# Pooled attention and a gated MLP on one core: another order of issue for the same blocks, and other engines for the steps that can stand on either of two

## The chip, the core and the metric

The kernel runs on one core of one Trainium2 chip. The metric is the time of one execution on the device in microseconds, of which less is better. The engines are named as in the profile: PE (TensorE: matmuls), PEld (its weight loads), DVE (VectorE), ACT (ScalarE), POOL (GpSimd) and SP (SyncE, which only issues transfers here). Each engine works through its own queue in the order in which the instructions were issued, and waits on semaphores for the others.

## What is computed

Attention over keys and values that are averaged by eight, for 8 batches, 8 heads, 576 rows and 64 columns a head; then on its output, read as 576 x 512 for each batch, a gated MLP that mixes rows with a 576 x 576 matrix. The weights arrive as 64-bit floats.

```python
def _attn_ref(q, k, v):
    k_p = k.reshape(B, H, Sp, pool, D).mean(axis=3)
    v_p = v.reshape(B, H, Sp, pool, D).mean(axis=3)
    scores = scale * np.matmul(q, k_p.transpose(0, 1, 3, 2))
    attn = np.exp(scores - np.max(scores, axis=-1, keepdims=True))
    attn = attn / (np.sum(attn, axis=-1, keepdims=True) + 1e-09)
    return np.matmul(attn, v_p)

def _moe_ref(x, w_in, g_ln, w_sg, b_sg, w_out):
    h = gelu_tanh(x @ w_in)
    u, v = h[..., :d_ff // 2], h[..., d_ff // 2:]
    v_n = (v - mean(v)) / np.sqrt(var(v) + 1e-06) * g_ln
    v_s = np.einsum('ts,bsd->btd', w_sg, v_n) + b_sg[None, :, None]
    return x + (u * v_s) @ w_out
```

## The kernel before

Nothing in the kernel loops over batches at run time: one program of 9779 profiled instructions is laid out in full. Its work is cut into steps, each a generator function with stages that end at a `yield`. A step has a letter, a number (the pair of heads g, a row tile i, or a column block d or m) and a batch b. The table `ORDER` (L27) names steps as `S2+3` (step S, pair 2, batch 3); `emit` (L770) goes through it and each time issues the next stage of that step. At the end every instruction is tied to the one before it on its engine, so the table is the order of issue on all engines and SyncE's queue. Where this text writes S2+3, it means that step.

The steps of a batch: A, B, C and E issue the loads of `kraw` (keys), `vraw`, `qT` and the values left over; K sums keys by eight into the block-diagonal `kbd`; P does so for the values (`vb` in batch 0, `vbh` and `vbl` later). S (L473) makes the scores of a pair of heads by five matmuls into a PSUM tile `aps`, the negated row maximum `nmax` (L486), the exps `e` and their sum `ssum`, and normalises. L and T transpose `e` and `el` (batch 0 on TensorE, later on VectorE and by a round trip of `tfar` through HBM) and split the result into a high part `ah` and a low part `al`. V multiplies with the values and copies PSUM to `xhl` and `x32` (named `x` in rows). J (batch 0) and H (a tile of 128 rows; H4 the 64 left over) make the v half of the first product, a gelu `vg`, its mean and variance, and the high and low parts `vhh`, `vhl` (`vht` for H4). U makes the u half. W (L684) mixes rows with `wsh`, `wsl`, `wth`, `wtl` and gates (`u`, L697, then `ghi` and `glo`). O multiplies with `w_out` (`woh`, `wol`) and adds `x` (L733, L721 in the last step). Z stores. Lower-case names are for the weights: `lv0` loads, `v0` to `v3`, `u0` to `u3`, `o0` to `o3` turn 64-bit words into a high and a low part (L275 to L283 and L222 to L231), `s0` to `s4` split the mixing matrix.

Two PSUM tiles `mps` go round between J, H, U, W and O, and two tiles `aps` between S, V and the transposes of batch 0; a step whose turn has come waits until the tile's last reader is done.

Some steps can stand on either of two engines. A key such as `m30` (kind of step, batch up to a cap, number) in the set `OTHER` takes the second:

```python
def copy(o, i, key):        # G ghi, h and x: V's copies, g vhh, s, T, P: VectorE if in OTHER, else ScalarE
def move(o, i, key):        # X, c: GpSimd if in OTHER, else ScalarE
def lower(o, x, y, key):    # with lowest: VectorE in one instruction if in OTHER, else ScalarE and GpSimd
def combine(o, x, y, op, key):  # V, H, W, s?d, v?d and the like: VectorE if in OTHER, else GpSimd
def sum8(o, t, key):        # k, p, l: one reduction on VectorE if in OTHER, else three sums on GpSimd
```

For the softmax three more: with `m` in `OTHER`, `soften` (L446) subtracts the maximum of the whole tile on VectorE (L448), `expo` (L451) is one exp on ScalarE (L453) and `total` (L460) one sum on VectorE (L462); without it, `expo` is ten exps with their own maximum and sum (L457), each followed by a read of the accumulator. With `n`, GpSimd normalises `e` (L443), without it VectorE, with the reciprocals kept in PSUM. With `z`, VectorE centres and scales `vg` in one instruction (L467), without it ScalarE does (L470, L471).

Exp and gelu lie in different tables of ScalarE. `ready` (L201) issues a one-column activation `early` (L204) where the function changes, with a table load ahead of it; how often that happens is set by the order.

Of the kernel before, what the change touches and what calls it, by code (L numbers as in the profile page):

```python
# [32 lines left out]
S0+1 J2+0 J3+0 H0+0 V3+0 C1+1 K1+1 o1 K0+2 C3+1 S1+1 H2+0 H2+0 C2+1 S2+1 K0+2 H0+0 H2+0 H1+0 s3 H0+0 H3+0 V1+0 H0+0
o0 s0 o0 H4+0 H2+0 H2+0 H0+0 S1+1 s1 H2+0 H3+0 o3 H4+0 B0+2 U0+0 H1+0 S2+1 H4+0 C0+2 S1+1 o2 A1+2 H3+0 o3 S2+1 o2 o2
S1+1 S1+1 U0+0 S0+1 o2 U1+0 U1+0 C1+2 o3 T0+1 P2+1 H1+0 H3+0 T0+1 S2+1 H4+0 S3+1 S3+1 S3+1 S0+2 o3 P2+1 S2+1 H4+0
T1+1 C2+2 U2+0 U2+0 S3+1 S3+1 s4 U3+0 S1+2 H3+0 H3+0 H4+0 H1+0 H1+0 L0+1 H4+0 H4+0 s4 T0+1 T2+1 U3+0 P2+1 S0+2 W0+0
W0+0 W0+0 S0+2 K1+2 L0+1 W1+0 W0+0 B1+2 P2+1 L0+1 W1+0 W1+0 L0+1 T0+1 W2+0 W2+0 P0+2 V0+1 V0+1 S1+2 P1+2 S1+2 W2+0
W2+0 T1+1 T1+1 L0+1 W3+0 W1+0 W3+0 O0+0 T1+1 V1+1 W3+0 C3+2 W3+0 T2+1 V1+1 V1+1 V1+1 T3+1 K1+2 S0+2 A0+3 S1+2 O1+0
O1+0 T2+1 T2+1 O0+0 O0+0 S2+2 V2+1 S0+2 V2+1 T0+2 T3+1 A1+3 O1+0 V2+1 E0+2 P2+2 O2+0 O3+0 S2+2 V0+1 S2+2 S2+2 T3+1
K0+3 S3+2 T3+1 O3+0 V2+1 O2+0 S3+2 S2+2 O2+0 V3+1 V3+1 V3+1 H0+1 H0+1 O3+0 Z3+0 H0+1 C1+3 H0+1 H1+1 H2+1 V3+1 S3+2  # L40
C0+3 H1+1 H1+1 S3+2 T0+2 T1+2 H0+1 H3+1 H2+1 S1+2 H0+1 K0+3 S0+3 H2+1 V0+1 Z2+0 H1+1 K1+3 H1+1 H4+1 S3+2 H3+1 H2+1
P2+2 H1+1 U0+1 L0+2 H4+1 H4+1 H3+1 H4+1 H4+1 T0+2 P2+2 P2+2 U1+1 U0+1 S1+3 L0+2 H3+1 Z0+0 H2+1 U1+1 C3+3 U2+1 S0+3
T0+2 P2+2 B0+3 L0+2 L0+2 H3+1 L0+2 V0+2 H4+1 H4+1 U3+1 T1+2 U2+1 U3+1 H2+1 H3+1 C1+4 H4+1 W0+1 T2+2 C2+3 S1+3 T1+2
S0+3 Z1+0 T1+2 V1+2 V0+2 T2+2 S1+3 W1+1 W0+1 V0+2 V1+2 V1+2 C0+4 K1+3 T3+2 P0+3 V0+2 S1+3 B1+3 A0+4 S2+3 T2+2 T2+2
S0+3 W1+1 V2+2 S2+3 S2+3 V2+2 V2+2 T3+2 K0+4 W2+1 W2+1 P1+3 E0+3 T3+2 S0+3 T0+3 W1+1 W1+1 W3+1 S3+3 T3+2 V3+2 W3+1
V3+2 V3+2 H0+2 W0+1 H0+2 T0+3 H1+2 K0+4 W0+1 T1+3 S3+3 S3+3 W2+1 H1+2 H2+2 S2+3 P2+3 V2+2 H2+2 C0+5 V1+2 W2+1 O0+1
W3+1 P2+3 S3+3 H0+2 T0+3 P2+3 P2+3 W3+1 S3+3 T0+3 V3+2 T2+3 P2+3 B0+4 S0+4 O0+1 O0+1 O1+1 O1+1 S2+3 S1+3 L0+3 O2+1
O2+1 H1+2 H0+2 H2+2 A1+4 H0+2 O1+1 H1+2 P0+4 H2+2 H1+2 H1+2 S1+4 H0+2 H3+2 O2+1 S0+4 S1+4 H3+2 L0+3 O3+1 C3+4 H3+2
H2+2 H4+2 L0+3 L0+3 C1+5 H4+2 A0+5 O3+1 V0+3 Z1+1 Z2+1 O3+1 H4+2 H4+2 Z0+1 C2+4 K1+4 Z3+1 E0+4 H4+2 S0+4 S0+4 U0+2
U0+2 U1+2 U1+2 H3+2 B1+4 T1+3 S0+4 T1+3 T1+3 H3+2 U2+2 H3+2 U2+2 P1+4 K0+5 H4+2 V1+3 H4+2 U3+2 T2+3 T2+3 L0+3 T3+3  # L50
U3+2 H2+2 V0+3 V0+3 H4+2 V1+3 S1+4 V0+3 P2+4 A1+5 W0+2 W1+2 T2+3 V2+3 W0+2 T3+3 W1+2 W1+2 V1+3 T3+3 V2+3 V2+3 V1+3
W2+2 T3+3 W3+2 W2+2 B0+5 W3+2 K1+4 K0+5 W2+2 W3+2 W1+2 V3+3 S2+4 T0+4 P2+4 V3+3 V3+3 H0+3 S1+4 S2+4 H1+3 H0+3 W0+2
W2+2 K1+5 H1+3 H1+3 H0+3 S2+4 W0+2 S3+4 H1+3 H1+3 S3+4 H2+3 H2+3 H2+3 W3+2 O0+2 O1+2 S1+4 O0+2 S2+4 S2+4 T0+4 T0+4
O0+2 O1+2 S0+5 S3+4 S3+4 O2+2 S1+5 T1+4 O2+2 S0+5 H2+3 S0+5 O1+2 H3+3 S3+4 L0+4 P2+4 T2+4 P0+5 H0+3 H1+3 V3+3 B1+5
H0+3 O2+2 H0+3 H3+3 H3+3 H3+3 H3+3 O3+2 O3+2 A0+6 T0+4 O3+2 V2+3 P2+4 Z2+2 S0+5 Z3+2 H4+3 H4+3 H4+3 L0+4 H4+3 H4+3
L0+4 U0+3 Z0+2 U0+3 P2+4 U1+3 L0+4 K0+6 V0+4 Z1+2 T1+4 S0+5 U1+3 K1+5 C2+5 L0+4 T3+4 S1+5 S1+5 S1+5 U2+3 U2+3 H3+3
T1+4 H2+3 U3+3 T1+4 V1+4 H2+3 U3+3 H4+3 E0+5 C1+6 C3+5 T2+4 P1+5 V0+4 V0+4 H4+3 T0+5 T2+4 H4+3 W0+3 W1+3 V1+4 W0+3
# [778 lines left out]
```

## Time and profile before

| | |
|---|---|
| median of 3 runs | 600.14 us (599.07 to 603.17) |
| the profiled execution, on the device | 599.96 us |
| its span, first to last instruction | 598.3 us |
| mean granted clock of TensorE | 0.973 |
| busy: PE, PEld | 546.6 us (91%), 506.7 us (85%) |
| busy: DVE, ACT, POOL | 415.6 us (69%), 318.4 us (53%), 274.2 us (46%) |
| moved by DMA | 67.10 MB |
| table loads on ACT | 43 at L204, 1283 ns each |

A timeline row gives the start and length in microseconds, the engine, the line, the operation, the tile written and the tiles read, the shapes and the number of like instructions merged; in brackets stands how long the engine had been idle and what ended that wait. A row by kind gives the count, then the busy time, the mean of one in ns, and the idle time ahead of it. Shares of the whole span are means over stretches with different limits, so the rows below go by stretch.

### The profile page before, as it was taken

The page shows a single profiled execution, that of the slowest core. Times are in us where ns is not written, and L with a number is a line of the kernel's source. Part 1 is how long each engine was busy: PE and PEld are TensorE (multiplying, and loading weights), DVE is VectorE, ACT ScalarE, POOL GpSimd, SP SyncE. Part 2 cuts the span into 40 slices and gives each one's busy share as a digit, 9 for nine tenths or more (in the row PEclk, how much of TensorE's full clock was granted, in tenths as well). Part 3 has the DMA queues.
Part 4 walks back from the last instruction along what each step waited for, and adds up shares of the span by engine and source line. Part 5 has one row for each costly group of instructions (what it writes and reads, how often), then busy time and mean ns, then how long its engine had stood idle before and what let it go on. Part 6 is the DMA issues. An engine that isn't in the chain of part 4 may idle for free. (4 is left out here: it accounts for less than half of the span.)

```text
span 598.3 us, 9779 instructions
## 1 busy us (share of the span) xinstructions
PE 546.6 (91%) x3552; PEld 506.7 (85%) x3552; DVE 415.6 (69%) x637; ACT 318.4 (53%) x833; POOL 274.2 (46%) x341
## 2 busy tenths in 40 slices
...
GB/s 288 389 173 60 146 114 80 135 121 127 92 207 132 66 125 253 81 93 16 178 169 100 76 65 157 133 85 99 82 132 31 79 1 101 79 100 40 1 1 80
DMA packets 43136, 67.10 MB, mean 112 GB/s; under 512 B 5776, under 2 KB 22160, under 8 KB 43088
## 3 DMA queue, kind: packets, MB, share of 16 engines
...
q10 hardware_dynamic: 288, 0.44, 0.3%
...
## 5 line engine op out<-in xcount | busy, mean ns | idle before, releaser
L133 PE MATMUL mps<-xhl,wih 128*128 128x288 f32 x512 | 91.2, 300 | 1.8 <-ACT u L681 1.1
L133 PE MATMUL mps<-wih,xhl 128*128 128x512 f32 x256 | 87.2, 410 | 5.0 <-DVE u L697 2.2
L133 PEld LDWEIGHTS mps<-xhl,wih 128*128 128x128 f32 x512 | 76.8, 192 | 3.4 <-ACT u L681 1.3
L443 POOL TENSOR_TENSOR e<-e,ssum 128x720 f32<-128x720 f32 x31 | 46.6, 1506 | 48.9 <-DVE ssum L442 33.9
L133 PEld LDWEIGHTS mps<-wih,xhl 128*128 128x128 f32 x256 | 49.4, 193 | 18.6 <-issue 2.0
L231 POOL TENSOR_TENSOR xhl<-x,xhl 128x576 fp32r<-128x576 f32 x23 | 35.5, 1550 | 58.4 <-ACT x L211 54.0
L133 PE MATMUL mps<-ghi,woh 128*128 128x288 f32 x240 | 53.3, 304 | 8.3 <-ACT vg L640 6.1
L457 ACT ACTIVATE e<-aps,nmax 128x72 f32<-128x72 f32 x180 | 54.7, 344 | 6.4 <-DVE nmax L486 6.3
L133 PE MATMUL mps<-xhl,wil 128*128 128x288 f32 x256 | 55.6, 298 | 0.0
L204 ACT ACT_TABLE_LOAD x43 | 55.2, 1283 | 0.7
L133 PE MATMUL mps<-wsh,vhl 128*128 128x288 f32 x256 | 55.0, 296 | 0.0
L133 PE MATMUL mps<-wsl,vhh 128*128 128x288 f32 x256 | 54.7, 295 | 0.0
L647 POOL TENSOR_TENSOR rstd<-mv,eps 128x1 f32<-128x1 f32 (+1 forms) x40 | 10.9, 274 | 95.4 <-DVE mv L645 84.0
L133 PE MATMUL mps<-wsh,vhh 128*128 128x288 f32 x256 | 54.6, 294 | 0.0
L133 PE MATMUL mps<-ghi,wol 128*128 128x288 f32 x240 | 52.0, 298 | 0.0
L133 PE MATMUL mps<-glo,woh 128*128 128x288 f32 x240 | 51.7, 297 | 0.0
L133 PE MATMUL mps<-wil,xhl 128*128 128x512 f32 x128 | 51.5, 403 | 0.0
L133 PEld LDWEIGHTS mps<-ghi,woh 128*128 128x128 f32 x240 | 39.1, 191 | 11.1 <-ACT vg L640 7.7
L695 DVE SCALAR_TENSOR_TENSOR mps<-mps,gcol,bbc 128x576 f32<-128x576 f32 x32 | 26.2, 817 | 27.0 <-PE mps L133 26.8
L231 POOL TENSOR_TENSOR glo<-u,ghi 128x576 fp32r<-128x576 f32 x15 | 24.6, 1649 | 42.1 <-ACT ghi L211 18.8
L644 DVE BATCH_NORM_STATS2 bst<-vg 128x6 f32<-128x512 f32 (+1 forms) x40 | 27.2, 680 | 23.1 <-ACT vg L640 21.1
L133 PE MATMUL aps<-kbd,qT 128*128 128x144 f32 x300 | 41.4, 286 | 1.6 <-ACT e L457 1.6
...
## 6 DMA issues: line engine op xcount, KB each, us to landing
qT<-in_q SPq DMA_DIRECT2D x31, 288.0 KB, 3.6
out<-x SPq DMA_DIRECT2D x31, 288.0 KB, 2.5
...
al<-tfar SPq DMA_DIRECT2D x28, 288.0 KB, 2.8
...
```

What stands on the lines that cost most here:

```text
L133: nc.tensor.matmul(o, lhsT, rhs, start=start, stop=stop)
L204: nc.scalar.activation(early, eps[:, 0:1], func)
L231: (nc.vector if key in OTHER else nc.gpsimd).tensor_tensor(o, x, y, op=op)
L443: (nc.gpsimd if key in OTHER else nc.vector).tensor_tensor(e, e, rec.unsqueeze(3).broadcast_to([P, NT, 2, SP]), op=ALU.mult)
L457: nc.scalar.activation(e[:, i, h], slots[i][:, h], AF.Exp, bias=nmax[:, i, h:h + 1], accum_out=ssum[:, i, h:h + 1])
L644: nc.vector.bn_stats(bst, vg)
L647: nc.gpsimd.tensor_tensor(rstd, mv[:, 1:2], eps[:n, 1:2], op=ALU.add)
L695: nc.vector.scalar_tensor_tensor(vs, vs, gcol[:, d:d + 1], bbc.rearrange("p (a n) -> p a n", a=2), op0=ALU.mult, op1=ALU.add)
```

## The change

Two tables are replaced: `ORDER`, with the same steps and stages in another sequence, and `OTHER`, from which 53 keys go and to which 43 come (104 instead of 114). No function is changed. A line of each table:

```diff
-E0+0 lv0 A0+0 A1+0 C0+0 C2+0 v0 H0+0 v0 v1 v1 K0+0 v0 v0 K1+0 K0+0 S0+0 S0+0 v1 v1 K1+0 C1+0 C3+0 S0+0 E0+1 P2+1
+A0+0 C0+0 E0+0 lv0 v1 v1 A1+0 K0+0 K0+0 S0+0 H0+0 H1+0 v1 C1+0 S1+0 B0+0 S0+0 K1+0 v1 S0+0 B1+0 A0+1 C2+0 S1+0 S1+0
-m30 m31 n00 n01 n02 n03 n10 n11 n12 n13 n20 n21 n22 n30 n31 n32 n33 o1d o1m o2a o2d o2m o3d o3m s2 s2d s3d s4 s4d
+c22 g00 g04 g10 g13 g14 g21 g22 g23 g24 h11 h20 k10 k31 l2 l3 m00 m02 m10 m12 m21 m22 m23 m30 m31 m32 m33 n00 n01
```

By engine: TensorE and SyncE keep their instructions. On ScalarE 150 of 200 single exps go and 15 whole-tile exps come; 14 table loads go, 29 stay; 15 casts of `ghi` come, 11 scalings of `vg` go. On VectorE 15 whole-tile subtractions and 15 sums come, 11 scalings of `vg`, 7 normalisations and 8 casts of `vhh` and `vht`; 15 casts of `ghi`, 13 low parts `vhl` and 5 casts of `xhl` go. On GpSimd 13 low parts `vhl` come and some parts of the weights; 7 normalisations go.

ScalarE's queue at the start, before (`top`, `wih`: parts of the weights; `kbd`: the keys of batch 0 or 1; `e`: exps; `ah`, `lt`, `vb`, `vl`: copies out of PSUM for batch 0):

```order
L275 ACTIVATE top<-raw 128x512 x2
L283 CAST wih<-top 128x512
L377 ACTIVATE kbd_96<-mps 64x2x72 x2
L228 ACTIVATE raw<-raw 128x512
L283 CAST wih<-top 128x512
L377 ACTIVATE kbd_96<-mps 64x2x72 x2
L457 ACTIVATE e,ssum<-mps,nmax 128x72 x10
L275 ACTIVATE top<-raw 128x512 x2
L457 ACTIVATE e,ssum<-mps,nmax 128x72 x10
L283 CAST wih<-top 128x512
L457 ACTIVATE e,ssum<-aps,nmax 128x72 x10
```

The same place of the changed kernel:

```order
L275 ACTIVATE top<-raw 128x512
L377 ACTIVATE kbd_96<-mps 64x2x72 x2
L228 ACTIVATE raw<-raw 128x512
L283 CAST wih<-top 128x512
L453 ACTIVATE e<-e 128x720
L457 ACTIVATE e,ssum<-mps,nmax 128x72 x10
L275 ACTIVATE top<-raw 128x512
L377 ACTIVATE kbd_96<-mps 64x2x72 x2
L377 ACTIVATE kbd_98<-kp 64x2x72 x2
L228 ACTIVATE raw<-raw 128x512
L283 CAST wih<-top 128x512
L275 ACTIVATE top<-raw 128x512
```

The first scores now stand ahead of the second half of batch 0's keys, and the first tile is one exp instead of ten; only one weight block's conversion stands ahead of them.

ScalarE's queue where the gelus of batch 2 (`vg`) and the scores S3+3 meet, before:

```order
L204 ACT_TABLE_LOAD
L204 ACTIVATE early<-eps 128x1
L640 ACTIVATE vg<-mps 128x512
L377 ACTIVATE kbd_96<-kp 64x2x72 x2
L204 ACT_TABLE_LOAD
L204 ACTIVATE early<-eps 128x1
L457 ACTIVATE e,ssum<-aps,nmax 128x72 x10
L204 ACT_TABLE_LOAD
L204 ACTIVATE early<-eps 128x1
L640 ACTIVATE vg<-mps 128x512 x2
```

and in the changed kernel:

```order
L204 ACT_TABLE_LOAD
L204 ACTIVATE early<-eps 128x1
L640 ACTIVATE vg<-mps 128x512 x3
L217 CAST xta<-xhl 128x128
L558 CAST ah<-al 128x576
L204 ACT_TABLE_LOAD
L204 ACTIVATE early<-eps 128x1
L453 ACTIVATE e<-e 128x720
```

Three gelus now follow each other, and S3+3 is one exp behind them instead of ten between the first and the second.

SyncE's last transfers, before and after in one piece of each queue (`x_5556` and `x_5292` hold the last batch's output; 128x288 is the first half of Z3+7, whose second half ScalarE issues). Before:

```order
L234 DMA al<-tfar 128x576
L234 DMA out<-x_4788 128x576 x3
L234 DMA out<-x_5556 128x576 x3
L234 DMA out<-x_5556 128x288
```

In the changed kernel:

```order
L234 DMA out<-x_4613 128x576 x3
L234 DMA out<-x_5292 128x576
L234 DMA out<-x_4613 128x576
L234 DMA out<-x_5292 128x288
L234 DMA out<-x_5292 128x576 x2
```

The half tile that stood last now stands ahead of two whole tiles (Z0+7 and Z2+7).

## Rows read from the trace of the kernel before

**Rows 1.** Busy time by stretch: window, length, busy per engine (instructions), clock, DMA share, GB/s.

```profile
22.90:105.40 82.50, 67.48 (x350) 55.48 (x350) 78.00 (x112) 64.82 (x218) 61.18 (x60) 0.88 0.42 138
107.00:594.60 487.60, 465.54 (x3145) 438.03 (x3143) 329.69 (x514) 246.39 (x602) 203.02 (x253) 0.99 0.33 98
193.90:200.70 6.80, 5.49 (x15) 4.62 (x16) 5.93 (x9) 2.12 (x3) 4.83 (x6) 0.50 0.26 68
```

**Rows 2.** Waits of PE from 107 to 595 us: us, times, longest.

```profile
PE mps L133 <- ACT vg L640: 7.3, 5, 2.5
PE aps L133 <- DVE al L561: 7.0, 7, 3.3
PE mps L133 <- DVE u L697: 3.6, 3, 1.6
PE mps L133 <- DVE xhl L231: 1.4, 1, 1.4
PE mps L133 <- DVE x L733: 1.1, 3, 0.7
PE mps L133 <- DVE vht L663: 1.0, 2, 0.8
```

**Rows 3.** Timeline of ACT and PE near 207 us.

```profile
204.02 0.30 ACT L457 ACTIVATE e<-aps,nmax 128x72 f32<-128x72 f32 x1
...
207.15 1.28 ACT L204 ACT_TABLE_LOAD   x1
...
208.56 1.06 ACT L640 ACTIVATE vg<-mps 128x512 f32<-128x512 f32 x2
...
209.19 0.54 PE L133 MATMUL mps<-ghi,woh 128*128 128x288 f32 x2 [2.16 <-ACT vg L640]
```

**Rows 4.** Timeline of ACT and DVE near 189 us.

```profile
188.46 0.69 ACT L211 CAST xhl<-aps 128x576 fp32r<-128x576 f32 x1
...
189.17 0.76 DVE L209 COPY x<-aps 128x576 f32<-128x576 f32 x1 [3.73 <-ACT xhl L211]
```

**Rows 5.** Timeline of the first 25 us, all engines.

```profile
8.62 1.22 ACT L275 ACTIVATE top<-raw 128x512 f32<-128x512 f32 x2 [6.33 <-DMA raw<-in_moe_w_in]
...
10.76 1.86 PE L133 MATMUL mps<-pool,kraw 128*128 128x16 f32 x8 [10.76 <-DMA kraw<-in_k]
...
20.09 4.24 PE L133 MATMUL mps<-kbd,qT 128*128 128x144 f32 x20
...
22.89 0.91 DVE L486 TENSOR_REDUCE nmax<-mps 128x10 f32<-128x720 f32 x1 [8.02 <-PE mps L133]
```

**Rows 6.** Timeline of DVE and PE at the end of W0 of batch 0.

```profile
105.42 1.05 DVE L231 TENSOR_TENSOR wtl<-stail,wth 64x576 fp32r<-64x576 f32 x1
...
106.52 0.53 PE L133 MATMUL mps<-wtl,vht 128*128 128x288 f32 x2
```

**Rows 7.** Kinds of instructions of ACT: count, busy us, mean ns, idle before.

```profile
L204 ACT ACT_TABLE_LOAD x43 | 55.2, 1283 | 0.7
...
L453 ACT ACTIVATE e<-e 128x720 f32<-128x720 f32 x12 | 9.7, 811 | 2.5 <-DVE e L448 2.5
...
L204 ACT ACTIVATE early<-eps 128x1 f32<-128x1 f32 x43 | 8.7, 203 | 0.5
```

**Rows 8.** Kinds of instructions of DVE, for whole-tile exps.

```profile
L448 DVE TENSOR_TENSOR e<-aps,nmax 128x720 f32<-128x720 f32 x12 | 10.9, 908 | 0.5
L462 DVE TENSOR_REDUCE ssum<-e 128x10 f32<-128x720 f32 x12 | 10.8, 897 | 6.8 <-ACT e L453 6.8
```

**Rows 9.** L278 by itself (min/median/max ns), and the kind `vhl` of POOL.

```profile
L278 DVE SCALAR_TENSOR_TENSOR top<-raw,top x12: 693/1348/1798, 9.8 to 87.2; 128x512 int32<-128x512 int32 x12
...
L231 POOL TENSOR_TENSOR vhl<-vg,vhh 128x512 fp32r<-128x512 f32 x3 | 4.2, 1410 | 0.2
```

**Rows 10.** The last issue (timeline), and stores of the page (KB each, us to landing).

```profile
595.44 0.35 ACTq L234 DMA_DIRECT2D out<-x  x1
...
out<-x SPq DMA_DIRECT2D x31, 288.0 KB, 2.5
```

More of the change, by code (lines that the diff above doesn't have):

```diff
@@ L33 @@
[L33 to L57, printed above, removed]
@@ new lines @@
+V1+1 T2+1 O0+0 O1+0 T2+1 S3+2 T0+2 T2+1 O1+0 V2+1 S2+2 P1+2 S1+2 E0+2 O2+0 T3+1 O2+0 O1+0 S3+2 S1+2 S1+2 T3+1 T3+1
+V2+1 O3+0 O3+0 Z1+0 O2+0 K0+3 V1+1 O3+0 V3+1 V3+1 V3+1 V2+1 H0+1 H1+1 T0+2 S3+2 S2+2 H0+1 T0+2 V2+1 S3+2 C0+3 T1+2
+V3+1 A1+3 C2+3 S0+3 S3+2 H0+1 L0+2 V1+1 H1+1 H1+1 P2+2 B0+3 H2+1 P2+2 P2+2 H0+1 L0+2 H2+1 H0+1 T0+2 S0+3 P2+2 H3+1
+H4+1 H0+1 H3+1 L0+2 H1+1 H1+1 P2+2 H1+1 K1+3 L0+2 K1+3 S1+3 U0+1 Z0+0 V0+2 H3+1 H4+1 H4+1 U1+1 U0+1 C1+4 H2+1 B1+3
+H3+1 H4+1 H2+1 T3+2 U1+1 L0+2 T1+2 Z3+0 Z2+0 U2+1 H3+1 U3+1 P0+3 H4+1 H4+1 T2+2 S1+3 T1+2 T1+2 V1+2 H2+1 U2+1 P1+3
@@ new lines @@
+U3+1 H2+1 A0+4 H3+1 V0+2 H4+1 H4+1 A1+4 W0+1 T2+2 S0+3 K1+4 W1+1 W0+1 T2+2 K0+4 V0+2 T2+2 E0+3 V1+2 V2+2 W1+1 W0+1
+S2+3 V2+2 V1+2 V2+2 S2+3 C3+3 S0+3 T3+2 T3+2 T3+2 W2+1 K0+4 V3+2 S0+3 S1+3 T0+3 T0+3 S3+3 S1+3 V3+2 W3+1 W2+1 V3+2
+H0+2 W3+1 V3+2 W1+1 W3+1 W2+1 V0+2 S2+3 S2+3 W0+1 W1+1 W3+1 S1+3 W2+1 P2+3 P2+3 P2+3 H0+2 H1+2 H1+2 H2+2 H0+2 C0+4
+H2+2 C2+4 V2+2 T0+3 B0+4 S3+3 S0+4 H1+2 T1+3 T2+3 S0+4 S2+3 S3+3 P2+3 O0+1 O0+1 S3+3 S3+3 O1+1 H0+2 O0+1 Z0+1 O1+1
+O1+1 P2+3 T0+3 H1+2 O2+1 H0+2 O2+1 V1+2 S1+4 L0+3 H2+2 L0+3 H1+2 H0+2 O2+1 H1+2 H3+2 S0+4 H3+2 H4+2 S0+4 S0+4 S1+4
```

77 lines of the change are left out of this document (46 added, 31 removed).

## The prediction

> **What bounds the kernel now.** Read three things. First the busy time by stretch [rows 1]: from 107 us to the last matmul TensorE is busy 465.54 of 487.60 us, so there it is the bound and only its 22.1 idle us can be won. Before that it is not: between 22.9 and 105.4 us TensorE works 67.48 of 82.50 us, but VectorE works 78.00 of 82.50, with 112 instructions that follow each other. The opening is VectorE's: the splitting of the weights (L277 to L231), the scores of batches 0 and 1, and the norms of batch 0 all stand in its one queue.
>
> Second, who ends TensorE's waits after 107 us [rows 2]: 7.3 us wait for a gelu (ACT vg L640) to free a PSUM tile, 7.0 for the low part of transposed weights (DVE al L561), 3.6 for the gating product (DVE u L697), 1.4, 1.1 and 1.0 for the rest: 21.4 us in all.
>
> Third, look into the long ones. Before the wait that ends at 209.19, ScalarE runs ten exps one by one from 204.02, then loads a table at 207.15, and the gelu that TensorE needs starts at 208.56 [rows 3]; TensorE has stood 2.16 us. Further back the same block of ten sits in front of a PSUM copy: ScalarE reaches `xhl` only at 188.46, and VectorE, which has to copy after it, has idled 3.73 us [rows 4]; what is then late is VectorE's queue behind that copy, and in it the low part `al` whose wait is the longest of its row, 3.3 us [rows 2]. After that wait the clock falls to 0.50 (1.2 GHz) from 193.9 to 200.7 [rows 1].
>
> **The change, part by part.** The work is the same on TensorE, on the DMA queues and in its sizes; its matmuls only come in another order. What moves between engines is counted from the order of issue, and priced by means.
>
> *The opening.* The first half of `kraw` is now issued first. Before, TensorE's first matmul waited for it until 10.76 us, with the weights' 1 MB ahead of it, which landed at 8.62 [rows 5]. So 512 KB took 2.1 us, some 245 KB per us. Now 512 KB and the 256 KB of `in_kv` come first, and 288 KB of `qT` beside them from ScalarE's queue: by that rate 3.1 to 4.3 us after the 3.4 us at which the first bytes must have begun (8.62 less 1280/245). I take 7.0: 3.8 us earlier. Each of the two K steps takes 4.7 us ((20.09 - 10.76)/2 [rows 5]); before, both stood ahead of the first scores, now one does, with ScalarE's copy of 0.6 between. First scores start at 12.3 instead of 20.09, and VectorE's first maximum at 15.1 instead of 22.89: 7.8 us earlier.
>
> That is not yet a gain, since VectorE bounds the stretch, and four or five instructions that it did ahead of the maximum now stand behind it. From the first maximum to the last low part of `vht` of batch 0 I count 112 instructions before and 115 after. Each priced by the mean of its kind, they make 81.8 and 84.0 us (the same three scores more with whole-tile exps, and the softmax normalised on VectorE, about +8; weights' parts and copies given to GpSimd and ScalarE, -8; the rest +2). The 81.8 stands against 82.5 us that passed, so such a sum is a fair clock here. If VectorE never waits in the new order, it is done at 15.1 + 84.0 = 99.1; before, the end of this stage was the low part `wtl`, finished at 106.47, for which the last matmuls of W0 waited until 106.52 [rows 6]; `wtl` now goes to GpSimd, ahead of need. But it will wait: v0's shift stands behind ScalarE's ten exps (1.7 us), v2's behind the copy of `vb`, which in the new queue waits for all of P0's matmuls (1.5), the first low part of `x` behind its own copies (0.9). With these 4.1 us it is done at 103.2, so the opening gives **-3 us**. Bounds: -7 if nothing waits, +1 if the waits are twice that.
>
> *ScalarE after the opening.* A block of ten exps, with an accumulator read after each, took 3.1 us in the block shown (204.02 to the table load at 207.15) [rows 3]. One whole-tile exp is 0.81 us [rows 7]. Twenty score steps had blocks of ten, five have now; after 107 us it is thirteen and one or none. Table loads fall from 43 to 29, each 1.28 us and a gelu or exp of one column of 0.2 [rows 7]. ScalarE has some 30 us less to do there. It isn't the bound, so none of this counts by itself; it counts where a block stood ahead of something that TensorE wanted. I can put 2.16 and 2.46 us (the longest of the gelu row, 2.5) and 3.26 us (the longest `al`, 3.3) on blocks of ten [rows 2 to 4]: 7.9 us. In the new order batch 3's `S3` stands between gelus with three O steps of matmuls in between, not one gelu away. Some of the smaller gelu waits go too, about 1 us.
>
> *VectorE after the opening* gets what ScalarE loses: 0.91 for each `e` that it now subtracts and 0.90 for its sum [rows 8], and loses casts of `ghi` to ScalarE and low parts `vhl` to GpSimd; by means +10 us on 329.69 [rows 1]. It stays far below TensorE, but scores now hold its queue for 1.8 us at a time and the waits for `al`, `u` and `xhl` are its own. I put +3 us on that. Together **-6 us** of waits; bounds -13 (three fifths of the waits gone) and, below, a loss.
>
> *GpSimd* takes 13 more `vhl`, 1.41 us each [rows 9], and gives up 7 normalisations. Between the H matmuls of a tile and the W that reads it there stand at least 16 us of other matmuls in the new order, against a chain of some 5 us, so I cost it at nothing; if that cover were gone each batch would pay the difference.
>
> *The clock.* In the 6.8 us at 0.50 TensorE was busy 5.49 [rows 1], of which half, 2.7 us, was lost. Without the 3.26 us wait ahead of it the clock should not fall there; another wait may put it elsewhere. **-1.5 us**, bounds -3 and +3.
>
> *The end.* Z0 and Z2 of batch 7 are now issued on SyncE behind the first half of Z3, which waits for the last addition. Before, the last issue was a half tile at 595.44 [rows 10] and the kernel ended at 598.3. Now two more issues of about 0.4 each follow, of 288 KB, which take 2.5 us at the median [rows 10] where they ran alone. **+1.3 us**, bounds +0.4 and +2.
>
> Sum against the profiled execution of 599.96 us (which is 0.2 below the median of the runs, 600.14): -3 - 6 - 1.5 + 1.3 = -9.2, so **590.8 us**.
>
> **The rivals.** *The opening pays for GpSimd.* VectorE's L278 takes 693 ns at best and 1798 at worst, median 1348 [rows 9], and the long ones lie where GpSimd is at work. Up to W0, GpSimd has about 6.4 us more to do by the same means (78.2 against 71.8). If all of it lengthens VectorE, the opening is +3.4 instead of -3, and the sum 599.96 + 3.4 - 6 - 1.5 + 1.3 = 597.2: no change that can be told. Against it, the 84.0 us are priced by means that already hold such delays. The Trainium skill says this as a rule (SBUF — State Buffer, "Who interferes with whom"): a VectorE instruction with two SBUF inputs and a GpSimd instruction that reads SBUF exclude each other for the whole instruction. By that rule, the min and the max of L278 are the free and the blocked case, and the trace agrees.
>
> *The waits move to VectorE.* Slower: TensorE's waits for VectorE after 107 us are now 7.0 + 3.6 + 1.4 + 1.1 + 1.0 = 14.1 us [rows 2]. If the longer blocks of the scores double them, while 7.9 us on ScalarE go, and the waits take the clock down once more (+3), the sum is 599.96 - 3 - 7.9 + 14.1 + 3 + 1.3 = 607.5. It decides from the point where VectorE's waits pass some 25 us. For it: its in-order queue; against it: 68% busy, and three PSUM tiles of the old order were asked for again within 1.4 us of matmuls after their last one, in the new order none within 2 us.
>
> *All of it lands:* opening -7, waits -13, clock -3, end +0.8: 577.8.
>
> **How the numbers follow.** About 1% (6 us) is what a measurement of this kernel can tell from no change. Forecast and its better side, 0.62 (0.08 of it below 577); the opening pays, or half of the waits return, 0.23; waits on VectorE, 0.15, two thirds of it above 606. So faster 0.62, same 0.23, slower 0.15, and 577 to 606 leaves out 0.18.
>
> **What would show it.** In the changed profile: the first matmul near 7 us, VectorE's first maximum near 15; VectorE without gaps up to 103; the first W0 done near 103.5; table loads 29; no ACT vg wait over 2 us after 110 us, and TensorE's waits there near 15 to 16 us; the clock at 1.00 near 195; two stores of 288 KB issued after the last addition. It is wrong if VectorE's `al`, `u` and `xhl` waits sum above 20 us, or if VectorE's opening holds over 8 us of gaps.

## The result, and the profile after

The changed kernel took 582.0 us (median; 580.68 to 582.64) where the kernel before took 599.75 beside it: a ratio of 0.969 (95% interval 0.9649 to 0.9731), 3.1% faster. The forecast was 590.8, and the range of 577 to 606 held it. The direction was right and the gain about twice as large as foreseen.

The profiled execution took 582.18 us, 17.8 less than that of before. Its page, busy time of each engine, share of the span and instructions:

```profile
PE 538.5 (93%) x3552; PEld 502.9 (87%) x3552; DVE 429.4 (74%) x639; ACT 270.2 (47%) x533; POOL 280.3 (48%) x350
```

and by stretch, with the columns of [rows 1]:

```profile
14.50:104.90 90.40, 67.89 (x365) 56.21 (x363) 85.76 (x115) 60.56 (x160) 65.28 (x65) 0.92 0.49 162
106.30:575.30 469.00, 461.77 (x3154) 438.03 (x3153) 339.66 (x517) 204.34 (x358) 207.27 (x258) 0.99 0.34 100
103.70:110.50 6.80, 5.57 (x23) 5.58 (x24) 6.16 (x11) 6.73 (x40) 3.22 (x5) 0.50 0.54 143
175.40:178.80 3.40, 3.40 (x17) 3.40 (x16) 2.39 (x5) 0.79 (x2) 0.49 (x1) 0.51 0.95 327
193.90:200.70 6.80, 6.80 (x40) 6.03 (x39) 6.14 (x13) 3.56 (x6) 3.07 (x4) 1.00 0.66 179
```

TensorE's waits after the first W0, which answer to [rows 2] (us in total, times, longest); these seven rows are all:

```profile
PE mps L133 <- DVE x L733: 2.0, 2, 1.4
PE aps L133 <- DVE al L561: 1.9, 3, 0.7
PE aps L133 <- DVE e L448: 1.5, 1, 1.5
PE mps L133 <- DVE xhl L231: 0.8, 2, 0.5
PE mps L133 <- DVE vht L663: 0.2, 1, 0.2
PE aps L133 <- DVE lt L540: 0.2, 1, 0.2
PE mps L133 <- POOL glo L231: 0.2, 1, 0.2
```

Three pieces make up the 17.8 us. Up to the end of W0+0 it is 0.8 (107.05 us before, 106.25 now). From there to the last matmul it is 18.5 (487.5 before, 469.0 now): TensorE's idle time fell from 22.0 to 7.2, by 14.8, and its busy time by 3.8 (465.54 [rows 1] to 461.77). The tail behind the last matmul grew by 1.5 (3.70 to 5.16). No wait for a gelu (ACT vg) is left, and the waits for VectorE, 14.1 us before, are 6.6, although VectorE now has more to do there than before: 339.66 us in 469 against 329.69 in 487.6 [rows 1].

The opening and the end, from the timeline:

```profile
6.29 1.86 PE L133 MATMUL mps<-pool,kraw 128*128 128x16 f32 x8 [6.29 <-DMA kraw<-in_k]
...
14.57 0.91 DVE L486 TENSOR_REDUCE nmax<-mps 128x10 f32<-128x720 f32 x1 [1.87 <-PE mps L133]
...
96.89 0.53 PE L133 MATMUL mps<-wsh,vhh 128*128 128x288 f32 x2 [1.62 <-ACT u L681]
...
101.80 0.53 PE L133 MATMUL mps<-wsh,vhl 128*128 128x288 f32 x2 [1.73 <-DVE vhl L231]
...
104.93 0.85 PE L133 MATMUL mps<-wth,vht 128*128 128x288 f32 x2 [2.60 <-DVE vht L663]
...
575.32 0.82 DVE L721 TENSOR_TENSOR x<-aps,x 128x288 f32<-128x288 f32 x2 [2.42 <-PE aps L133]
575.86 1.30 SPq L234 DMA_DIRECT2D out<-x  x3
```

The first matmul and the first maximum come 4.5 and 8.3 us earlier than in [rows 5], and yet the first W0 ends where it did. At the end, three stores leave SyncE behind the first half of the last addition instead of one: the half tile of 144 KB and two whole ones of 288 KB.

### The profile page after: what moved, and what is told of

The parts are those of the page before. It is cut to its first block, busy times and chain, and to the rows that moved or that the text cites. A ratio compares the mean times of both kernels' runs of the same rounds, so it can differ in the third digit from the quotient of the medians.

```text
span 580.5 us, 9490 instructions
## 1 busy us (share of the span) xinstructions
PE 538.5 (93%) x3552; PEld 502.9 (87%) x3552; DVE 429.4 (74%) x639; ACT 270.2 (47%) x533; POOL 280.3 (48%) x350
## 4 chain that ended last, share of the span: by engine, by line
PE 59%; DVE 26%; DMA 4%; POOL 4%; issue 3%; ACT 2%; SPq 1%; DVEq 0%; POOLq 0%; ACTq 0%
PE mps L133 50%; PE aps L133 9%; DVE nmax L486 2%; DVE top L278 2%; DVE e L448 1%; SPq L234 1%; DVE ssum L462 1%; DVE bst L644 1%; DVE xhl L231 1%; DVE raw L279 1%; DVE al L561 1%; DVE top L231 1%; DMA al<-tfar 1%; DVE y L509 1%; DMA kraw<-in_k 1%
## 5 line engine op out<-in xcount | busy, mean ns | idle before, releaser
L133 PE MATMUL mps<-wih,xhl 128*128 128x512 f32 x256 | 84.4, 400 | 3.7 <-DVE xhl L231 2.4
L443 POOL TENSOR_TENSOR e<-e,ssum 128x720 f32<-128x720 f32 x24 | 35.9, 1499 | 61.6 <-DVE ssum L442 61.6
L133 PEld LDWEIGHTS mps<-wih,xhl 128*128 128x128 f32 x256 | 47.7, 188 | 16.1 <-DVE xhl L231 3.9
L133 PE MATMUL mps<-wsh,vhh 128*128 128x288 f32 x256 | 56.5, 303 | 1.6 <-ACT u L681 1.6
L133 PE MATMUL mps<-ghi,woh 128*128 128x288 f32 x240 | 51.6, 295 | 2.0 <-DVE x L733 2.0
L647 POOL TENSOR_TENSOR rstd<-mv,eps 128x1 f32<-128x1 f32 (+1 forms) x40 | 10.2, 255 | 86.1 <-DVE mv L645 84.4
L231 POOL TENSOR_TENSOR xhl<-x,xhl 128x576 fp32r<-128x576 f32 x23 | 32.9, 1435 | 34.2 <-ACT x L211 30.6
L133 PE MATMUL aps<-kbd,qT 128*128 128x144 f32 x300 | 43.4, 293 | 1.9 <-ACT x L211 1.7
L133 PEld LDWEIGHTS mps<-wsh,vhh 128*128 128x128 f32 x256 | 42.4, 195 | 1.9 <-ACT u L681 1.8
L133 PEld LDWEIGHTS mps<-wsh,vhl 128*128 128x128 f32 x256 | 42.3, 194 | 2.0 <-DVE vhl L231 2.0
L133 PEld LDWEIGHTS aps<-kbd,qT 128*128 128x128 f32 x300 | 40.3, 194 | 3.6 <-ACT x L211 2.4
```

The costliest lines, as they stand in the source:

```text
L133: nc.tensor.matmul(o, lhsT, rhs, start=start, stop=stop)
L231: (nc.vector if key in OTHER else nc.gpsimd).tensor_tensor(o, x, y, op=op)
L443: (nc.gpsimd if key in OTHER else nc.vector).tensor_tensor(e, e, rec.unsqueeze(3).broadcast_to([P, NT, 2, SP]), op=ALU.mult)
L647: nc.gpsimd.tensor_tensor(rstd, mv[:, 1:2], eps[:n, 1:2], op=ALU.add)
```

## The experiments

Each run's times, in one table. "W0" is the end of the last matmul of W0+0 with `wtl`, "stretch" the time from there to the last matmul, "idle" TensorE's gaps in it, all three from the run's profile. Ratios are against the kernel before, run beside it on the same chip, and compare better from row to row than the medians.

| run | against | median us | ratio (95%) | W0 | stretch | idle |
|---|---|---|---|---|---|---|
| before | | 600.14 | 1 | 107.1 | 487.5 | 22.0 |
| changed | | 582.0 | 0.969 (0.965 to 0.973) | 106.3 | 469.0 | 7.2 |
| e1, new engines alone | before | 649.3 | 1.080 (1.075 to 1.084) | 127.2 | 517.5 | 41.8 |
| e2, new sequence alone | before | 611.9 | 1.019 (1.012 to 1.025) | 115.6 | 488.7 | 23.6 |
| e3, whole exps alone | before | 596.2 | 0.992 (0.989 to 0.996) | 108.7 | 484.2 | 17.4 |
| e4, stores first | changed | 579.1 | 0.963 (0.959 to 0.967) | 106.4 | 466.1 | 6.2 |
| e5, five blocks of ten back | changed | 579.3 | 0.966 (0.962 to 0.969) | 106.5 | 464.9 | 5.8 |
| e9, e4 and e5 | changed | 579.4 | 0.963 (0.958 to 0.968) | 106.1 | 468.2 | 6.5 |
| e6, ghi and vhl back | changed | 588.7 | 0.982 (0.978 to 0.986) | 107.1 | 473.6 | 13.3 |
| e11, ghi back | changed | 584.6 | 0.972 (0.967 to 0.977) | 106.2 | 471.5 | 9.3 |
| e12, vhl back | changed | 587.9 | 0.977 (0.971 to 0.982) | 107.1 | 474.1 | 13.0 |
| e13, engines of batches 2 to 7 back | changed | 599.8 | 0.999 (0.996 to 1.002) | 104.7 | 486.2 | 18.5 |
| e14, engines of the opening back | changed | 592.7 | 0.986 (0.983 to 0.990) | 114.6 | 473.0 | 12.2 |
| e15, scaling and normalising back | changed | 582.0 | 0.969 (0.965 to 0.973) | 106.8 | 468.3 | 8.6 |
| e16, the other keys back | changed | 596.4 | 0.994 (0.991 to 0.997) | 105.8 | 484.0 | 17.9 |
| e17, five casts of xhl back | changed | 592.3 | 0.985 (0.980 to 0.991) | 107.5 | 479.6 | 14.9 |
| e18, vhh and glo back | changed | 591.1 | 0.983 (0.979 to 0.988) | 108.1 | 475.8 | 13.2 |
| e8, weights first | changed | 584.5 | 0.975 (0.971 to 0.979) | 110.4 | 466.8 | 7.0 |
| e7, two of o's steps to GpSimd | e4 | 578.3 | 0.965 (0.961 to 0.969) | 106.4 | 465.6 | 7.7 |
| e10, four steps to ScalarE | e9 | 581.1 | 0.966 (0.961 to 0.971) | 108.2 | 467.6 | 6.1 |

### Is it the engines or the sequence? (e1, e2, e3)

The theory at that point, A: short exps on ScalarE made the gain, so the new `OTHER` should bring most of it. The rival, B: the new sequence did.

```diff
 e1: before, with
-OTHER of before
+OTHER of the change, and n02
 e2: before, with
-ORDER of before
+ORDER of the change
+m21 m23 m32 n23
 e3: before, with
+m00 m10 m12 m21 m23 m32 m33
```

> The old order of issue with the new engines (one key, n02, stays as before). Theory A, the short exps on ScalarE did it: the gelu waits of 7.3 us and the long al wait of 3.3 us go although the steps stand as close as before; about 590 us, TensorE's waits after 107 us near 13 us, opening and end as before (first matmul 10.8 us). Theory B, the new spacing of the steps did it: the waits for al, u and xhl stay or grow with VectorE's 10 us more; 596 to 602 us, waits after 107 us of 18 us or more.

> The new order with the old engines (m21, m23, m32 and n23 stay as in the changed kernel; 13 blocks of ten exps instead of 5, five of them with the table loads of batches 3 to 7). Theory A: each of the six blocks after the opening can hold a gelu up, 2 us each at worst: 589 to 593 us, gelu waits of 5 us or more after 107 us. Theory B: the spacing absorbs them: 583 to 586 us, gelu waits under 2 us.

> The kernel before with seven more m keys alone: 15 score steps go from ten exps to one on ScalarE and two more instructions on VectorE; order, table loads (43) and all other engines as before. Theory A: 590 to 593 us, gelu waits from 7.3 to under 3 us. Theory B: 597 to 601 us; what ScalarE's waits lose, VectorE's gain.

Both theories fell. The new engines in the old sequence are 8% slower than before, the new sequence with the old engines 1.9% slower; only together are they 3.1% faster. The whole-tile exps alone bring 0.8%. The longest wait of TensorE in e1, and then in e2, each in the opening (line numbers of e2 and e3 are one higher):

```profile
77.74 1.30 PE L133 MATMUL aps<-ah,vb 128*128 128x288 f32 x2 [12.17 <-DVE e L443]
```

```profile
54.29 1.04 PE L177 MATMUL aps<-ident,el 128*32 128x128 f32 x4 [10.19 <-POOL el L504]
```

A step that stands well in one engine's queue stands behind something late in another's: in e1 VectorE works at the weights (L277 to L279 and L209) from 62.93 to 75.37 ahead of that `e`, and in e2 GpSimd has the sums of `vraw`, an `e` and an `xhl` ahead of `el`. e3's longest rows of TensorE's waits after W0:

```profile
PE aps L134 <- DVE al L562: 7.4, 10, 1.9
PE mps L134 <- DVE x L734: 3.5, 6, 1.6
PE mps L134 <- DVE u L698: 3.0, 2, 1.6
```

No wait for a gelu `vg` on ScalarE is left of the 7.3 us of [rows 2], so in the old sequence the blocks of ten did cause those; but `al` and `u` wait as long as before (7.0 and 3.6), `x` longer, and the idle time fell by 4.6 us only.

### What are the blocks of ten worth in the new sequence? (e5, and e4 and e9)

```diff
 e5: changed, with
-m33
 e4: changed, with Z0+7 and Z2+7 issued ahead of Z3+7
 e9: e4 and e5 together
```

> The changed kernel with one key less (m33): the scores of the fourth pair of heads in batches 3 to 7 are again ten single exps, as in the kernel before; 5 of the 13 blocks that became whole-tile exps after 107 us go back. ScalarE is held 3.1 us at such a place instead of 0.8, VectorE does 1.8 us less. Theory A (the gain after the first W0 comes from the short exps alone, wherever they stand): TensorE's waits there were 22.0 us before and 7.2 after the change; 5/13 of the difference returns, so 587 to 589 us, with ACT vg or POOL/DVE rows behind the ten exps. Theory B (the new sequence leaves so much between a score and what reads it that one long block no longer reaches TensorE): 580.5 to 583.5 us, and TensorE's waits after 106 us stay below 9 us.

> The changed kernel with the last stores Z0+7 and Z2+7 issued ahead of Z3+7. From the last matmul to the end of the span 5.16 us become 3.7 as in the kernel before: 580.6 us, all else as in the changed kernel. If the end is set by something else than SyncE's queue, 582 us.

> The changed kernel with both single edits that made it faster: the two whole stores ahead of the half one (579.1 us alone) and the last pair's scores of batches 3 to 7 as ten exps (579.3 alone). If the two lie in different places, as the traces say (the last 5 us; the stretch from 106 us to the last matmul), they add: 576 to 577 us. If the second was only another place of the half-clock stretches, as its trace's 1.5 us at 0.50 after the first W0 against 7.7 leaves open, it does not come again: 578.5 to 580 us.

Five of the thirteen blocks that the change took away after 107 us are back in e5, and TensorE's waits don't return: 5.8 us of idle time against 7.2. The median is even lower, but e9, with the same edit on e4, is no faster than e4. The stretches of e5 and e9 differ by 3.3 us, of which 0.7 is idle time and 2.6 busy time, and the time at half clock after W0 is 1.5 us in e5's profile and 7.6 in e9's (7.7 in the changed kernel's). So in this sequence these five long blocks on ScalarE cost nothing that can be measured, and theory A is gone for the later stretch.

e4 answers for the end. Its last issues:

```profile
573.03 0.33 SPq L234 DMA_DIRECT2D out<-x  x1
573.36 0.35 ACTq L234 DMA_DIRECT2D out<-x  x1
```

The tail is 3.65 us again, 1.5 shorter than in the changed kernel. That e4's last matmul also ends 2.8 us earlier is of the size in which e5 and e9 differ, and isn't claimed. So the changed kernel with its stores first is shorter than the changed kernel by the 1.5 us of the tail.

### Which stretch pays for whose engines? (e13, e14)

```diff
 e13: changed, with
-W21 X20 X21 g23 l2 m33 x20 x21 z22 z32 z33
+G22 G23 H20 H22 V23 W23 X22 X23 c20 h31 k20 n33 x22 z21
 e14: changed, with the 67 keys as before that differ for the weights and batches 0 and 1
```

> The changed kernel with the engines of before for the steps of batches 2 to 7 (all keys of those batches but m21, m23, m32 and n23), and the new engines for the weights and batches 0 and 1; the new sequence throughout. Run e2, which had the old engines everywhere, took 9.4 us longer up to the end of the first W0 and 19.7 us longer from there to the last matmul than the changed kernel. Theory S (the stretch after the first W0 pays for its own engines: what stands in VectorE's queue there ends TensorE's waits): the first W0 ends near 107 and the stretch behind it takes 480 us or more against 469: 592 to 600 us. Rival O (e2's long second stretch was carried over from its late opening): no more than e6, whose four keys are among these: 587 to 590 us.

> The complement of e13: the engines of before for the weights and for batches 0 and 1, the new ones for batches 2 to 7; the new sequence throughout. Theory S: the first W0 ends later by what e2 showed, 4 to 9.4 us (110 to 115.6), and the stretch behind it stays at 469 to 474 us: 586 to 595 us. Rival O: the late opening drags the stretch behind it to 480 us or more: 598 us or more.

With the old engines for batches 2 to 7 (but for four keys, m21, m23, m32 and n23) the opening is as in the changed kernel, even 1.5 us shorter, and the stretch behind it takes 486.2 us, as before the change. With the old engines for the opening, W0+0 ends 8.4 us later, and the stretch loses only 4.0. So the later stretch's whole gain hangs on its own engines, in the new sequence. Together the two lose what e2 loses (e13 17.2 us in the stretch, e14 8.4 and 4.0; e2 9.4 and 19.7). Windows of the two, first e13's stretch, then e14's opening and stretch:

```profile
104.70:590.90 486.20, 467.71 (x3155) 440.38 (x3153) 332.92 (x524) 214.55 (x450) 204.55 (x259) 0.99 0.33 97
```

```profile
14.80:109.30 94.50, 68.29 (x343) 57.54 (x343) 73.85 (x112) 60.93 (x198) 61.27 (x64) 0.84 0.46 153
114.60:587.60 473.00, 460.85 (x3155) 437.83 (x3153) 344.20 (x519) 203.43 (x356) 204.40 (x253) 0.99 0.34 99
```

In e13 VectorE has less to do (332.92 us) than in the changed kernel (339.66), and TensorE waits 11 us longer. In e14's opening VectorE works 73.85 of 94.5 us where it worked 85.76 of 90.4: the opening was VectorE's only as long as the other engines fed it in its sequence. Busy time does not tell which division is better.

e13's idle time is near that of the kernel before (18.5 and 22.0 us), but it is made of other waits. Some of e13's, after W0:

```profile
PE aps L133 <- DVE al L561: 3.5, 4, 1.1
PE mps L133 <- DVE xhl L231: 2.6, 3, 1.8
PE mps L133 <- DVE vhl L231: 2.2, 2, 2.1
PE mps L133 <- DVE vhh L209: 2.2, 2, 1.8
PE mps L133 <- POOL glo L231: 1.9, 2, 1.5
PE mps L133 <- ACT vg L640: 1.3, 2, 1.0
```

Against [rows 2] the waits for `vg` fell from 7.3 to 1.3, those for `al` from 7.0 to 3.5, and those for `u` (3.6) are gone; the waits for `vhl`, `vhh` and `glo` stand in no row there. The new sequence takes the old waits away and brings others, and the new engines take those away: in the changed kernel 7.2 us are left.

### Which steps of the later stretch? (e6, e11, e12, e15 to e18)

```diff
 each: changed, with
+G22 G23 H20 H22                                        (e6)
+G22 G23                                                (e11)
+H20 H22                                                (e12)
-z22 z32 z33  +z21 n33                                  (e15)
-W21 X20 X21 g23 l2 x20 x21  +V23 W23 X22 X23 c20 h31 k20 x22   (e16)
+h31                                                    (e17)
-g23 W21  +W23                                          (e18)
```

> The changed kernel with G22, G23, H20, H22 as before: from batch 2 on, VectorE again casts ghi for two of four column blocks and makes the low part vhl of two tiles; 24 instructions, some 16 us more on VectorE after the first W0 (340 us of 470), and as much less on ScalarE and GpSimd. Theory C (the whole-tile exps pay because VectorE was emptied for them; its one queue is what TensorE waits for): TensorE's waits for al, x, xhl and u grow by 4 us or more, 586 to 592 us. Rival (VectorE at some 76% still has cover in the new sequence): 580.5 to 583.5 us.

> The changed kernel with G22 and G23 as before: 12 casts of ghi in batches 2 to 7 go from ScalarE back to VectorE, 0.41 us or more each; half of what e6 did, which cost 6.7 us. Theory L (a GpSimd instruction stands in VectorE's way for its time, so work given to GpSimd is not won, but work given to ScalarE is): this half carries the cost, 585 to 588 us. Theory Q (VectorE's own busy time counts, wherever the work came from): 5 of the 15 us that e6 added are here, so some 2 us of the cost, 583.5 to 585.

> The changed kernel with H20 and H22 as before: 12 low parts vhl of batches 2 to 7 go from GpSimd (1.4 us each) back to VectorE (0.65 to 0.9 each); the other half of e6. Theory L: GpSimd no longer blocks VectorE for them, so VectorE's gain and loss cancel: 581.5 to 583.5 us. Theory Q: 10 of the 15 us that e6 added are here, some 4.5 us of its cost, 586 to 588.

> The changed kernel with two kinds of step of batches 2 to 7 as before: vg of tiles 2 and 3 is scaled by VectorE and ScalarE in two instructions instead of one on VectorE (z21 for z22, z32, z33), and e of the last pair is normalised by GpSimd (1.5 us) instead of VectorE (0.9 us) (n33). Of the 17.2 us by which e13 lengthened the stretch after the first W0, e6's four keys explain some 7 and the ten exps nothing; some 10 are open. Theory Z (these two shorten the chain from a gelu or an exp to what TensorE reads, at VectorE's cost): they carry most of the 10, 588 us or more. Rival R (the rest of the keys, whose run is e16): 581 to 584 us. Rival J (no key carries it alone, all together make VectorE's queue late): 583 to 586 us in both.

> The changed kernel with the remaining keys of batches 2 to 7 as before: W23 for W21 (glo of another column block on VectorE), V23, X22, X23, x22 for X20, X21, x20, x21, c20, h31, k20, and without g23 and l2: copies and parts of which most are only batch 2's; h31 gives a cast of xhl per batch from 3 on to VectorE, g23 takes a cast of vhh of tile 3 per batch from VectorE. Theory R (these carry the open 10 us of e13): 588 us or more. Theory Z (e15's keys carry them): 581 to 584 us. Rival J: 583 to 586 us in both.

> The changed kernel with one key of e16 alone (h31): five casts of xhl of the second pair, one in each of batches 3 to 7, read from PSUM by VectorE again instead of ScalarE. e16's lag against the changed kernel grows by some 6 us in batch 3, and by 3 to 4 us in batches 4 and 5, and its trace has TensorE waiting 1.98 us for an xhl of VectorE at 268 us. Theory H (each such cast stands behind what VectorE has in its queue, and the PSUM tile of V1 comes free that much later): most of e16's 14.4 us, 590 to 596 us. Rival G (vhh and glo, run e18, carry it): 581 to 584 us. Rival J (they act together): 583 to 588 in both.

> The changed kernel with e16's two other kinds of step that come in every batch: vhh of tile 3 is cast by ScalarE instead of VectorE (no g23), and glo of column block 3 instead of 1 is made by VectorE (W23 for W21), the other by GpSimd. Theory H (h31, run e17, carries it): 581 to 584 us. Rival G: 590 to 596 us, with TensorE waiting for vhh or for POOL's glo. Rival J: 583 to 588 us in both.

By the ratios, `ghi` on VectorE costs 0.3% (2 us, within the intervals and so not shown), `vhl` 0.8% (4.6 us), both 1.3%; all as theory Q had it; theory L fell here, since giving `vhl` to GpSimd did pay: on VectorE two of these low parts end waits of TensorE in e12's profile, 3.4 us in sum, and none does in the changed kernel. e15's keys cost nothing (rival R). e16's cost 2.5%, and of them the five casts of `xhl` alone (e17) 1.6%, about 10 us, and the casts and low parts of e18 1.4%. Theory H's figure for e17 and rival G's for e18 both came. Their sum, 3.0%, is more than e16's 2.5%, but the intervals, 0.3 to 0.6% to either side, don't tell whether the two overlap. The keys of e5, e6, e15 and e16 make up those of e13: their prices are -0.3, 1.3, 0 and 2.5%, 3.5% in sum, where e13 costs 3.0%.

How five casts of 0.76 us cost 10 us is seen in the first of them. e17, VectorE and TensorE:

```profile
240.96 0.76 DVE L209 CAST xhl<-aps 128x576 fp32r<-128x576 f32 x1 [9.36 <-PE mps L133]
241.64 0.74 DVE L467 SCALAR_TENSOR_TENSOR vg<-vg,mv,rstd 128x512 f32<-128x512 f32 x1
242.41 0.43 DVE L209 CAST vhh<-vg 128x512 fp32r<-128x512 f32 x1
...
244.56 0.54 PE L133 MATMUL mps<-wsh,vhh 128*128 128x288 f32 x2 [2.05 <-DVE vhh L209]
246.61 0.85 PE L133 MATMUL mps<-wsh,vhl 128*128 128x288 f32 x2 [1.25 <-POOL vhl L231]
```

and the same place of the changed kernel, VectorE and ScalarE:

```profile
232.07 0.74 DVE L467 SCALAR_TENSOR_TENSOR vg<-vg,mv,rstd 128x512 f32<-128x512 f32 x1
232.85 0.43 DVE L209 CAST vhh<-vg 128x512 fp32r<-128x512 f32 x1
...
241.50 0.64 ACT L211 CAST xhl<-aps 128x576 fp32r<-128x576 f32 x1 [1.96 <-PE mps L133]
```

The cast waits for TensorE's V1+3 in both. On VectorE it holds up, for 9.36 us, the scaling and the cast `vhh` of batch 2, which the changed kernel does at 232; they come at 242, batch 2's other casts and low parts come behind them, and the W that reads them waits 2.05 and 1.25 us. Then the clock is at 0.50 for 3.4 us, from 246.4. On ScalarE, where it waits 1.96 us, TensorE has no wait behind it in the changed kernel before 260 us. e13, whose keys have these casts on VectorE too, shows the same place:

```profile
236.95 0.76 DVE L209 CAST xhl<-aps 128x576 fp32r<-128x576 f32 x1 [9.35 <-PE mps L133]
```

The kernel before has the same five casts on VectorE, but in its own sequence the longest wait of one is 2.4 us (at 453.0), and no wait of TensorE for a `vhh` stands in [rows 2]. So 10 us is the price of these casts in the new sequence, and not what they cost before; the same holds for the prices of the other keys in this section. By the times of L733, which ends each O step, e17 lags behind the changed kernel by -0.6 us when O of batch 1 is done and by 4.7 when O of batch 2 is, by 6.3, 10.4 and 11.8 after batches 3, 4 and 5, and by no more from there on, so the last of the five casts cost nothing.

### What sets the end of the opening? (e8, e7, e10)

```diff
 e8: changed
-A0+0 C0+0 E0+0 lv0 v1 v1
+E0+0 lv0 A0+0 C0+0 v1 v1
 e7: e4, last stages of o2 and o3 behind s4, and
-o2a o2d o2m o3a
 e10: e9, with
-s2 s3 g00 m12
```

> The changed kernel with its first loads in the sequence of before: E0+0 and the weights lv0 ahead of A0+0 and C0+0, all else as changed. The first matmul should come at about 10 us (6.3 in the changed kernel), the first maximum of VectorE at about 18.3 (14.57). Theory V (VectorE works without gaps from its first maximum to the end of the opening, so its start moves its end): the first W0 ends 3 to 4 us later, 585 to 586 us. Rival S (the early start is slack that something later takes up, such as the weights, which then land earlier): 581 to 583 us.

> The changed kernel with its stores first (579.1 us by itself), and with the last stages of o2 and o3 behind s4 and on GpSimd (o2a, o2d, o2m, o3a): VectorE loses four instructions, 5.7 us, of its queue ahead of vht of batch 0 (94.6 to 99.6 us and one at 103.5), ScalarE gains 0.6, GpSimd about 5.5, after wtl. Theory V (VectorE's queue sets the end of the opening): the first W0 ends 4 to 5.5 us earlier, 573.5 to 575.5 us. Rival L (a VectorE instruction with two inputs from SBUF waits for GpSimd's reads, so what GpSimd gets VectorE loses): VectorE's instructions from 95 to 105 us grow longer, 578 to 580 us. Rival T (TensorE or ScalarE is the next bound right behind VectorE): 576.5 to 578.

> The kernel of the run before (e9) with four keys less in the opening: two casts of the mixing matrix (s2, s3) and the cast vhh of tile 0 of batch 0 (g00) go from VectorE to ScalarE, and the scores S2+1 become ten exps (m12), which takes the subtraction and the sum from VectorE. VectorE loses 1.36 + 0.43 + 0.91 + 0.84 = 3.5 us ahead of the first W0, ScalarE gains 4.3, and GpSimd keeps its work. Theory L (VectorE's queue sets the end of the opening, and e7 gained nothing only because GpSimd's instructions stand in VectorE's way): the first W0 ends 2.5 to 3.5 us earlier than 106.4, and the time is 2.5 to 3.5 us below e9's, near 573.5. Rival D (VectorE isn't what sets that end, which is why e7 gained nothing): within 1 us of e9.

e8 went as theory V said for the opening: VectorE's first maximum comes 3.25 us later (17.82), and W0+0 ends 4.2 later. The time rose by 0.6%, 3.5 us; the intervals of the two ratios overlap, so it is the profile's W0+0 that tells.

e7 took 5.7 us of instructions from VectorE's queue and won nothing: W0+0 ends at 106.36. VectorE and GpSimd in e7:

```profile
94.89 2.43 DVE L470 SCALAR_TENSOR_TENSOR mv<-mv,rstd 128x1 f32<-128x1 f32 x1
97.25 2.95 DVE L428 SCALAR_TENSOR_TENSOR vbl<-vp,head,vbh 128x256 fp32r<-128x256 f32 x2
101.57 1.76 DVE L467 SCALAR_TENSOR_TENSOR vg<-vg,mv,rstd 64x512 f32<-64x512 f32 x1
...
94.65 1.61 POOL L231 TENSOR_TENSOR wtl<-stail,wth 64x576 fp32r<-64x576 f32 x1
96.20 1.05 POOL L224 TENSOR_TENSOR raw<-raw 128x512 f32<-128x512 f32 x1
97.19 1.28 POOL L231 TENSOR_TENSOR top<-top,woh 128x512 f32<-128x512 f32 x1
98.55 1.37 POOL L231 TENSOR_TENSOR wol<-raw,top 128x512 fp32r<-128x512 f32 x1
```

and the same three instructions of VectorE in the changed kernel:

```profile
94.49 0.15 DVE L470 SCALAR_TENSOR_TENSOR mv<-mv,rstd 128x1 f32<-128x1 f32 x1
...
99.55 0.87 DVE L428 SCALAR_TENSOR_TENSOR vbl<-vp,head,vbh 128x256 fp32r<-128x256 f32 x2
...
101.67 0.73 DVE L467 SCALAR_TENSOR_TENSOR vg<-vg,mv,rstd 64x512 f32<-64x512 f32 x1
```

These three grew by 2.28, 2.08 and 1.03 us, and with the smaller ones by 5.8 in all: what GpSimd got, VectorE lost beside it, theory L's mechanism. VectorE's instruction on one column starts beside GpSimd's `wtl` and ends where GpSimd's second instruction ends, at 97.3. The Trainium skill warns of it (Perfetto Trace Analysis, "Optimizing Scalar/DVE Operations"): work moved between these two might not help, for they share a port. e7 agrees with 5.7 us moved and nothing won; e12 shows the other side, where the same kind of move is worth 4.6 us.

e10 took 3.5 us from VectorE without touching GpSimd, and W0+0 ended 2.2 us later than in e9. Its VectorE:

```profile
82.68 1.23 DVE L231 TENSOR_TENSOR vhl<-vg,vhh 128x512 fp32r<-128x512 f32 x1 [2.96 <-ACT vhh L211]
...
90.55 0.90 DVE L277 TENSOR_SCALAR top<-top 128x512 int32<-128x512 int32 x1 [2.19 <-ACT top L275]
```

The cast `vhh`, now ScalarE's, stands behind ten exps of S1+1, and the next weight block behind the new ten of S2+1. VectorE waits 5.2 us for them, more than the 3.5 it was spared; in e9 VectorE waits for neither. So e10 doesn't tell theory L from rival D; it shows a third thing, which e17 shows too.

## Why the prediction was right or wrong, step by step

**The mechanism it saw was real and small.** The steps that carried the -6 were three long waits behind blocks of ten exps. These waits are gone, the clock near 195 us is at 1.00 (2.4 GHz), and no gelu wait is left, as it said; table loads are 29. But e3 gives 0.8% for the exps in the old sequence, where the gelu waits went and `al` stayed, and e5 and e9 give nothing measurable for five blocks in the new one.

**The step that failed** is the term for the waits after 107 us: -6 forecast, with a bound of -13, and -14.8 measured. By whom TensorE waited for, the gelu waits gave -7.3, where the forecast had 2.16, 2.46 and about 1, and the waits for VectorE gave -7.5 (14.1 to 6.6), where it had 3.26 off for one `al` and 3 on for VectorE's longer queue, almost nothing in sum. So most of the miss is the price of VectorE's queue. It was set by how long an instruction lasts and on how busy an engine it lands, from waits of the old sequence. Its parts came out otherwise:
- "+3 us" for VectorE, which gets ten more: its busy time did rise by ten, and the waits for it fell by more than half.
- "I cost it at nothing" for the low parts `vhl` on GpSimd, since 16 us of matmuls cover a chain of 5. GpSimd's side did cost nothing (no wait for `vhl` is left), but in the new sequence the move is worth 4.6 us (e12), since VectorE is spared them.
- The casts of `xhl`, `vhh` and `ghi` got no price. In the new sequence five casts of `xhl` are worth about 10 us (e17).

e13 puts all of it together: with the old engines for batches 2 to 7, the stretch of the new sequence is as long as before, 486.2 us, with other waits. What the forecast lacked was a look, in the new sequence, at each instruction that waits for TensorE, and at what is ready behind it in the same queue. Both tables have to be read for that together, which e1 and e2 show: either alone loses.

**The opening** was put at -3 and is -0.8. The first matmul (6.29 for 7.0) and the first maximum (14.57 for 15.1) came as worked out. The sum of VectorE's work was 84.0 and is 85.76, its waits 4.1 and are 4.6; so it was done at 104.87, not at 103.2. The remaining half microsecond is the clock: the last matmuls of W0+0 ran at 0.50 (1.2 GHz; it fell at 103.7, within the wait of 2.60 us), and from the last low part to their end it took 1.38 us, where e7, at 1.00 there, took 0.84. That an earlier start is not yet a gain held: 8.3 us at the first maximum became 0.8 at the end.

**The clock** was put at -1.5. In the kernel before it fell at 193.9, within the 3.26 us wait, which ends at 195.21, and not after it; in the changed kernel it does not fall there, but it does at 175.4, 1.2 us behind the end of a wait of 1.53. Time at half clock after W0 fell from 10.2 to 7.7 us, of which about 1 us is TensorE's (2.5 us, busy four fifths, half of it lost). Of the 3.8 us that TensorE is less busy, some 2.7 are not explained.

**The end** was put at +1.3 and is +1.46, and e4 takes it back.

**The rivals.** That GpSimd's work is paid for by VectorE is shown in e7, where all of it was; in the change itself VectorE's busy time in the opening came out 1.8 us over its sum by means (85.76 for 84.0), where that rival had 6.4. The waits did not move to VectorE: rival two named its in-order queue, which is the right place, but the new division relieves it. "All of it lands" came closer with the waits (-13) and was wrong on the opening (-7), so that its 577.8 lies nearer to the result than the forecast is in part luck. So is the range of 577 to 606, which holds a time whose largest term lies outside its own bounds.

**What stays open:** how the keys share the later stretch's gain exactly; the 2.7 us of busy time; and why the old sequence with the new engines loses so much after its opening (517.5 us), which was not taken apart. e1's profile has 41.8 us of idle time there, 4.4 of it in one wait for GpSimd's `vhl`, and 30.7 us at half clock.
